# Plain f32 value products, one output bank, and side work in the gaps of an attention stage

## The chip, the cores and the metric

The kernel runs on one core of one Trainium2 chip. The metric is the time of one execution on the device in microseconds; the median of three runs is given.

## The reference, cut to what matters

```python
def _attn_ref(q, k, v):                       # q, k, v: 4 x 12 x 448 x 64, f32
    scores = scale * np.matmul(q, k.transpose(0, 1, 3, 2)) - np.log(S)
    attn = 1.0 / (1.0 + np.exp(-scores))
    return np.matmul(attn, v)
x = attn_out.transpose(0, 2, 1, 3).reshape(1792, 768)
h = x @ moe_w_in; x = elu(h) @ moe_w_out      # 768 -> 2048 -> 768
h = x @ moe2_w_in; out = (h - tanh(h)) @ moe2_w_out
```

A sigmoid takes the place of the softmax, so no row has to be normalised. The four weights arrive with 64-bit elements.

## The kernel before

**Attention.** 4 batches of 12 heads are 24 pairs of heads. For each pair `n`, TensorE transposes Q and K (`transpose`, keys `("t", n, w)`), and ScalarE and VectorE split the result into two fp32r parts whose sum is the f32 value (`head`, `rest`). Scores are then three fp32r products each. They come in four units: `u` = 0 to 2 are 128 keys of both heads at once, two 64-row halves side by side; `u` = 3 is the last 64 keys of both heads, stacked on 128 partitions. ScalarE takes the sigmoid out of PSUM (`sig`). The value products (`pv`) for `u` = 0 to 2 are plain f32, each head in 64 columns of the array. The one for `u` = 3 takes parts of sigmoid and V that were split as well (`ahead`, `arest` on VectorE, `vhead`, `vrest` on GpSimd) and is three fp32r products. VectorE copies the sum out (`xdone`). Score tiles and the transposes of the pair two turns ahead rotate through three tiles of two banks (`pss`); the value sums through two single banks (`psv`).

**The two layers.** They follow on the same tokens, in two sets (`s` = 0: 1024 tokens, `s` = 1: 768). Each layer's products go by Strassen's scheme: seven products of sums of quarters, with operands `B11, B21, T1, T2, B22, T3, T4` made from the attention output by `x_sum`, `x_head` (ScalarE) and `x_rest` (VectorE), in the places that `SLOTS` gives. Weights are narrowed from 64 bits to f32 in three steps (`narrow`, `p_narrow`: ScalarE, VectorE, VectorE). The output weights of the first layer are loaded, narrowed, summed (`p_sum`) and stored during attention (`p_load` to `p_store`, `j` = 0 to 7), four blocks of the input weights too (`load`, `narrow`, `keep`). All of this is called side work below.

**The order.** Nothing is ordered by the compiler. `Sched` holds every operation with a queue (PE, ACT, DVE, POOL, SP), a believed cost, a believed latency, what it follows and a rank. `emit` walks through time: it always takes the operation that can start first, the rank deciding between equals, and emits the program in the order of the starts so found. Each engine then runs its own operations in exactly that order, waiting on semaphores. For attention the order on each engine is fixed by `PHASES` (times within a turn of `CYCLE`) and `chain`; the products of the layers are one chain on TensorE. SyncE issues almost all DMAs, in order too.

```python
op("p_load", (j, c), "SP", 600, p_load, [("s", max(2 * j - 1, 0), 0)] + (was[c:c + 1] if wide else held), 6000)
...
raw_op(("load", n), "SP", 600, lambda: load(n, key, not live), after, 5400 if live else 3900)
```

The last number of each is the believed latency in nanoseconds.

Of the kernel before, what the change touches and what calls it, by code (L numbers as in the profile page):

```python
# [9 lines left out]
F32 = mybir.dt.float32  # L10
# [6 lines left out]
class Sched:  # L17
# [3 lines left out]
    def __init__(self):  # L21
        self.ops, self.before = {}, {}
# [8 lines left out]
    def emit(self):  # L31
        ops = self.ops
# [12 lines left out]
        while any(ready.values()):  # L45
            best = None
            for queue, keys in ready.items():
                t0 = free.get(queue, 0)
                for k, t in keys.items():
                    c = (max(t, t0), ops[k][4], str(k))  # L50
                    if best is None or c < best[0]:
                        best = c, queue, k
            (start, rank, _), queue, k = best
            del ready[queue][k]
            free[queue] = start + ops[k][1]
            done[k] = free[queue] + ops[k][5]
            order.append((start, len(order), ops[k][2]))
# [5 lines left out]
        for start, _, fn in sorted(order, key=lambda o: o[:2]):  # L63
            fn()
# [5 lines left out]
CYCLE = 6900  # L70

PHASES = {
    ("s", 0): 0, ("s", 1): 620, ("s", 2): 1240, ("s", 3): 1900, ("pv", 3): CYCLE + 2500,
    ("t", 1): 3100 - 2 * CYCLE, ("t", 0): 3500 - 2 * CYCLE, ("pv", 0): 4000, ("pv", 1): 4900, ("pv", 2): 5800,
    ("sig", 0): 700, ("sig", 1): 1700, ("sig", 2): 2700, ("sig", 3): 3700,
    ("head", 1): 4400 - 2 * CYCLE, ("head", 0): 5000 - 2 * CYCLE,
    ("ahead", 3): 4500, ("rest", 1): 5050 - 2 * CYCLE, ("arest", 3): 5100, ("rest", 0): 5700 - 2 * CYCLE,
    ("xdone",): CYCLE + 3300, ("vhead",): 1000, ("vrest",): 2000,
# [9 lines left out]
def kernel(  # L88
# [27 lines left out]
    NAN, NAH, NAF, NVL, NL = 6, 2, 2, 2, 2  # L116
# [27 lines left out]
    rooms = {tag: raw_p.tile([128, n], F32R if tag == "XA" else F32, tag=tag, name=tag) for tag, n in ROOMS.items()}  # L144
    raws = {(tag, 0): raw_p.tile([128, n], F32, tag=tag, name=tag) for tag, n in RAW.items()}
# [9 lines left out]
    with tc.manual_schedule():  # L155
# [7 lines left out]
        def attention():  # L163
# [7 lines left out]
            psv = [apool("psv0", 1, early, space=bass.MemoryType.PSUM, side="right")]  # L171
            psv += [apool("psv1", 1, space=bass.MemoryType.PSUM)]
# [4 lines left out]
            ah_p = apool("ah", NAH)  # L177
# [12 lines left out]

            vs = [vs_p.tile([128, 2, 2, D], F32R, name=f"vs{i}") for i in range(2)]
# [100 lines left out]
            def transpose(n, w):  # L292
                if ("tps", n) not in T:
                    T["tps", n] = pss[(5 * n - 6) % 3].tile([128, 2, BK], F32, tag="s", name="sps")
# [6 lines left out]
            def head(n, w):  # L301
                W, slot = ((S, 1), (512, 2))[w]
                nc.scalar.activation(out=es[n % 2][:, slot, :W], in_=T["t", n, w][:, :W], func=ACTF.Copy)  # L303
# [14 lines left out]
            def vhead(n):  # L318
# [1170 lines left out]
```

## Time and profile before

| what | value |
|---|---|
| median of three runs | 1041.16 us (1039.48 to 1042.59) |
| profiled execution | 1045.44 us, span 1043.7 us |
| TensorE matmul busy, share of the span | 998.7 us, 96% |
| VectorE busy | 779.1 us, 75% |
| ScalarE busy | 605.4 us, 58% |
| GpSimd busy | 108.8 us, 10% |
| bytes moved by DMA | 218.62 MB, mean 209 GB/s |

The span is the time from the first to the last instruction of the profiled execution. Busy shares are means over stages that differ: attention ends at about 196 us, the first layer lies up to about 625 us, the second behind it. Where TensorE is busy nearly throughout, the time of a stage is TensorE's; elsewhere one looks for what ended its idle time.

### The profile page before, as it was taken

The page shows a single profiled execution, that of the slowest core. Times are in us where ns is not written, and L with a number is a line of the kernel's source. Part 1 is how long each engine was busy: PE and PEld are TensorE (multiplying, and loading weights), DVE is VectorE, ACT ScalarE, POOL GpSimd, SP SyncE. Part 2 cuts the span into 40 slices and gives each one's busy share as a digit, 9 for nine tenths or more (in the row PEclk, how much of TensorE's full clock was granted, in tenths as well). Part 3 has the DMA queues.
Part 4 walks back from the last instruction along what each step waited for, and adds up shares of the span by engine and source line. Part 5 has one row for each costly group of instructions (what it writes and reads, how often), then busy time and mean ns, then how long its engine had stood idle before and what let it go on. Part 6 is the DMA issues. An engine that isn't in the chain of part 4 may idle for free.

```text
span 1043.7 us, 15621 instructions
## 1 busy us (share of the span) xinstructions
PE 998.7 (96%) x5276; PEld 865.4 (83%) x5276; DVE 779.1 (75%) x1135; ACT 605.4 (58%) x976; POOL 108.8 (10%) x122
## 2 busy tenths in 40 slices
PE   8887999989999999999999999899999999999998
PEld 5555666678888878888789998798898999999998
DVE  2766778797877778666878789788787788665673
ACT  4666778765556557554657655344444556445652
POOL 1001121121111110000000021132222000000000
PEclk8988999999999999999999999899999999999999
DMA  7989994044455559999995732555555895455443
GB/s 201 294 250 312 275 265 114 16 149 168 167 173 177 171 180 296 357 388 359 393 322 174 229 120 97 179 184 189 185 196 185 292 310 188 127 167 169 134 134 94
DMA packets 171264, 218.62 MB, mean 209 GB/s; under 512 B 58672, under 2 KB 129584, under 8 KB 170928
## 3 DMA queue, kind: packets, MB, share of 16 engines
q1 hardware_dynamic: 169616, 217.04, 62.9%
q8 instruction: 41, 0.67, 0.3%
q10 hardware_dynamic: 1568, 0.59, 0.2%
q14 instruction: 39, 0.32, 0.1%
HBM read 142.61 MB, written 74.97 MB: 208 GB/s over the span
## 4 chain that ended last, share of the span: by engine, by line
PE 55%; DMA 14%; DVE 12%; issue 4%; ACT 3%; SPq 1%; POOL 0%; DVEq 0%; ACTq 0%; POOLq 0%
PE psa L760 8%; PE psd L760 7%; PE psx L760 6%; DMA second<-in_moe_w_in_dram 5%; PE psu L915 4%; PE psw L915 4%; PE psv L915 4%; PE psa L915 3%; PE psb L915 3%; PE psb L760 3%; PE sps L333 3%; PE psx L915 3%; PE pvps L371 3%; DMA R1a<-in_moe_w_out_dram 2%; PE psy L915 2%
## 5 line engine op out<-in xcount | busy, mean ns | idle before, releaser
L333 PE MATMUL sps<-e 64*128 64x448 f32 (+1 forms) x504 | 74.3, 387 | 16.1 <-ACT an L347 12.8
L333 PEld LDWEIGHTS sps<-e 64*128 64x128 f32 (+1 forms) x504 | 51.7, 189 | 45.2 <-ACT an L347 20.3
L887 ACT ACTIVATE XB<-t 128x384 fp32r<-128x384 f32 (+1 forms) x111 | 61.7, 563 | 36.2 <-DMA t<-x_forms 13.5
L347 ACT ACTIVATE an<-sps,bias 128x896 f32<-128x896 f32 x72 | 67.8, 1006 | 25.4 <-PE sps L333 25.2
L891 DVE TENSOR_TENSOR XB<-t,XB 128x384 fp32r<-128x384 f32 (+1 forms) x111 | 68.0, 625 | 12.2 <-ACT XB L887 12.2
L675 POOL TENSOR_TENSOR second<-second 128x384 f32<-128x384 f32 x15 | 17.4, 1161 | 534.3 <-DVE second L562 273.7
L371 PE MATMUL pvps<-an,vl 128*64 128x448 f32 x288 | 61.7, 565 | 0.0
L760 PE MATMUL psd<-XB,R0a 128*128 128x512 f32 (+1 forms) x192 | 55.3, 369 | 4.3 <-ACT R1b L772 2.5
L760 PE MATMUL psa<-XB,W 128*128 128x512 f32 x192 | 55.2, 397 | 0.0
L887 ACT ACTIVATE XB<-spare 128x512 fp32r<-128x512 f32 (+1 forms) x72 | 40.7, 571 | 21.1 <-DMA spare<-x_forms 5.6
L891 DVE TENSOR_TENSOR XB<-spare,XB 128x512 fp32r<-128x512 f32 (+1 forms) x72 | 44.0, 621 | 6.3 <-ACT XB L887 6.3
L915 PE MATMUL psu<-XB,XB 128*128 128x384 f32 (+1 forms) x192 | 46.5, 349 | 1.4 <-DVE XB L880 1.4
L308 DVE TENSOR_TENSOR e<-sps,e 128x512 fp32r<-128x512 f32 (+1 forms) x48 | 31.2, 653 | 21.0 <-ACT e L303 19.5
L915 PE MATMUL psv<-XB,XB 128*128 128x384 f32 (+1 forms) x192 | 46.2, 348 | 0.0
L915 PE MATMUL psw<-XB,XB 128*128 128x384 f32 (+1 forms) x192 | 46.2, 348 | 0.0
L675 POOL TENSOR_TENSOR first<-first,second 128x384 f32<-128x384 f32 x30 | 43.9, 1463 | 1.2
L760 PEld LDWEIGHTS psa<-XB,W 128*128 128x128 f32 x192 | 37.0, 192 | 8.1
L760 PEld LDWEIGHTS psd<-XB,R0a 128*128 128x128 f32 x192 | 35.9, 192 | 9.0 <-ACT R1b L772 2.9
L371 PEld LDWEIGHTS pvps<-an,vl 128*64 128x64 f32 x288 | 19.2, 142 | 28.0 <-issue 23.8
L760 PE MATMUL psd<-XA,W 128*128 128x512 f32 x144 | 37.1, 403 | 3.3 <-DVE W L692 2.0
L915 PEld LDWEIGHTS psu<-XB,XB 128*128 128x128 f32 x192 | 34.6, 188 | 3.9 <-DVE XB L880 1.7
L793 ACT ACTIVATE spare<-spare 128x512 f32<-128x512 f32 (+1 forms) x64 | 36.5, 571 | 0.7
(359 smaller groups left out, 2698.8 us busy)
## 6 DMA issues: line engine op xcount, KB each, us to landing
x_forms<-R1b SPq DMA_DIRECT2D x58, 256.0 KB, 2.0
first<-p_forms SPq DMA_DIRECT2D x36, 384.0 KB, 6.5
t<-x_forms SPq DMA_DIRECT2D x64, 192.0 KB, 2.8
t<-x_forms SPq DMA_DIRECT2D x47, 256.0 KB, 4.9
x_forms<-t SPq DMA_DIRECT2D x44, 256.0 KB, 2.0
x_forms<-R1b SPq DMA_DIRECT2D x58, 192.0 KB, 5.6
first<-in_moe_w_in_dram SPq DMA_DIRECT2D x14, 768.0 KB, 5.7
second<-in_moe_w_in_dram SPq DMA_DIRECT2D x14, 768.0 KB, 7.3
```

The lines of the kernel that those rows point to most:

```text
L308: nc.vector.tensor_tensor(out=e[:, to, :W], in0=T.pop(("t", n, w))[:, :W], in1=f(e[:, slot, :W]), op=ALU.subtract)
L333: nc.tensor.matmul(out=ps[:, j, :S], lhsT=e[lanes, ks, cols], rhs=e[lanes, qs, :S], start=(x == 0), stop=(x == 2),)
L347: nc.scalar.activation(out=a[:, :m], in_=T.pop(("s", n, u))[:, :m, :S], func=ACTF.Sigmoid, bias=bias, scale=scale)
L371: nc.tensor.matmul(out=ps[D * j:D * j + D], lhsT=vl[n // NL % NVL][:, n % NL, 5 * j + u], rhs=a[:, j], start=(u == 0), stop=False,)
L675: by.tensor_tensor(out=out, in0=x, in1=y, op=op)
L760: nc.tensor.matmul(out=ps, lhsT=w[wz][:, k0:k0 + 128], rhs=xs[xz][:, kk], start=(opens and n == 0), stop=(n == 3 * KH - 1), skip_group_che ...
L793: nc.scalar.activation(out=r, in_=r, func=ACTF.Exp, scale=-1.0)
L887: nc.scalar.activation(out=at_place(og_place[i, s, p, j], 0, i)[:, :HW[s]], in_=T["graw", i, s, p, j], func=ACTF.Copy)
L891: nc.vector.tensor_tensor(out=lo, in0=T.pop(("graw", i, s, p, j)), in1=f(hi), op=ALU.subtract)
L915: nc.tensor.matmul(out=T["o2", tag], lhsT=lhsT, rhs=rhs, start=(p in OPENS and j == 0 and x == 0), stop=(j == NG - 1 and x == 2), skip_gro ...
```

## The change

- The value product of `u` = 3 becomes one plain f32 product of the sigmoid and V as loaded, in the pair's own turn. `ahead`, `arest`, `vhead`, `vrest` go, and their tiles.
- The copy `head` of Q (`w` = 0) moves from ScalarE to VectorE.
- PSUM: `u` = 3's scores get a bank of their own (`psq`); all pairs share one bank for the value sums (`psv`), so `pv` 0 of a pair follows `xdone` of the pair before. The ring `pss` has four uses a pair in place of five.
- The planner first plans attention alone (`emit(True)`). In the real planning an operation of ACT or DVE that is not in that plan is put off if it would end more than `GIVE` = 100 ns (beside the lateness that there is already) after the planned start of the next planned one.
- Believed latencies of transfers grow (`load` 8500 and 6000, `p_load` 11000, `p_store` 8000, and some loads of the layers). `p_load` no longer follows every second pair's scores, and narrowing no longer follows `head`.
- First operands of layer 1 are made in three pieces of one pair each; `XB2` is set aside from the start, and `T1`, `T2`, `B22` change places.

```diff
@@ planner
+                    if k not in plan and planned.get(queue) and c[0] + ops[k][1] > plan[planned[queue][-1]] + late + GIVE:
+                        c = (10 ** 9,) + c[1:]
...
+            start = max(ready[queue][k], free.get(queue, 0))
+            if k in plan:
+                late = start - plan[k]
...
+        if only_plan:
+            self.plan = {o[3]: o[0] for o in order}
+            return
@@ attention
-    NAN, NAH, NAF, NVL, NL = 6, 2, 2, 2, 2
+    NAN, NAF, NVL, NL = 3, 1, 2, 2
-            psv = [apool("psv0", 1, early, space=bass.MemoryType.PSUM, side="right")]
-            psv += [apool("psv1", 1, space=bass.MemoryType.PSUM)]
+            psq = apool("psq", 1, early, space=bass.MemoryType.PSUM, side="right")
+            psv = apool("psv", 1, space=bass.MemoryType.PSUM)
...
+                if w:
+                    nc.scalar.activation(out=to, in_=x, func=ACTF.Copy)
+                else:
+                    nc.vector.tensor_copy(out=to, in_=x)
...
-                    t = T.pop(("h", n, u))
-                    for vz, az in ((0, 0), (0, 1), (1, 0)):
-                        nc.tensor.matmul(
-                            out=ps, lhsT=vs[n % 2][:, vz], rhs=t[:, az], start=False, stop=(vz == 1)
-                        )
+                    nc.tensor.matmul(
+                        out=ps, lhsT=vl[n // NL % NVL][:, n % NL, 3:5], rhs=T.pop(("a", n, u))[:, 0], start=False, stop=True
+                    )
...
-                n, x = divmod(5 * n + x - 3, 5)
-                return [("sig", n, x)] if x < 4 else [("rest", n + 2, 0), ("rest", n + 2, 1)]
+                n, x = divmod(4 * n + x - 3, 4)
+                return [("sig", n, x)] if x < 3 else [("rest", n + 2, 0), ("rest", n + 2, 1)]
...
-                       + {0: loaded("v", n) + [("xdone", n - 2)], 3: [("vrest", n)]}.get(u, []))
+                    op("pv", n, (u,), "PE", 790, pv, [("sig", n, u)] + (loaded("v", n) + [("xdone", n - 1)] if u == 0 else []))
@@ layers
             def pieces(i, s):
-                return (slice(None),)
+                return (slice(None),) if i else range(KH)
...
-                raw_op(("load", n), "SP", 600, lambda: load(n, key, not live), after, 5400 if live else 3900)
+                raw_op(("load", n), "SP", 600, lambda: load(n, key, not live), after, 8500 if live else 6000)
...
-                            fixed[done] = (4 + 2 * n) * CYCLE
+                            fixed[done] = n * CYCLE
...
-                    op("p_load", (j, c), "SP", 600, p_load, [("s", max(2 * j - 1, 0), 0)] + (was[c:c + 1] if wide else held), 6000)
+                    op("p_load", (j, c), "SP", 600, p_load, [("s", 1, 0)] + (was[c:c + 1] if wide else held), 11000)
...
-                           [done] + (held + [("head", 2 * j + c + 2, 0)] if step == 0 else []), 100)
+                           [done] + (held if step == 0 else []), 100)
...
-            FIRST["XA2"] = FIRST["XB0"] = formed
+            ended = [[k for k in formed if k[1] == NG - 2 + u and (raw is None or k[0] == "p_narrow")] for u, raw in ((0, 1), (0, None), (1, 1), (1, None))]
+            FIRST["XB0"], FIRST["XA2"] = ended[0] + ended[1] + ended[3], ended[2]
...
         attention()
+        sch.emit(True)
         mlp()
         sch.emit()
```

## Rows read from the trace of the kernel before

**Rows 1.** Windows: stretch, length, busy PE, PEld, DVE, ACT, POOL, PEclk, DMA, GB/s.

```profile
10.21:189.77 179.56, 162.52 (x1004) 103.59 (x1003) 127.98 (x209) 127.44 (x177) 22.65 (x45) 0.93 0.80 240
11.30:18.20 6.90, 6.34 (x25) 3.96 (x25) 1.08 (x3) 4.83 (x7) 0.00 (x0) 0.51 0.82 184
...
51.40:56.50 5.10, 0.00 (x0) 0.00 (x0) 1.44 (x3) 2.59 (x4) 0.00 (x0) 0.92 0.78 178
56.50:62.50 6.00, 5.96 (x20) 4.27 (x22) 3.03 (x5) 3.97 (x6) 1.24 (x2) 0.50 0.75 240
...
94.46:101.16 6.70, 0.00 (x1) 0.00 (x0) 2.51 (x4) 3.66 (x6) 0.74 (x2) 0.66 0.93 301
101.16:106.90 5.74, 5.74 (x20) 4.10 (x22) 3.60 (x8) 3.70 (x6) 0.75 (x2) 0.50 1.04 343
...
196.14:225.00 28.86, 26.11 (x120) 22.70 (x119) 27.08 (x29) 21.28 (x32) 7.66 (x4) 0.94 0.19 69
217.10:223.00 5.90, 3.29 (x10) 2.74 (x9) 5.90 (x9) 4.50 (x9) 0.00 (x0) 0.71 0.49 191
...
20.00:160.00 140.00, 123.52 (x770) 79.75 (x771) 99.07 (x170) 97.17 (x134) 17.30 (x34) 0.94 0.91 281
160.00:196.00 36.00, 36.00 (x229) 22.14 (x228) 28.27 (x37) 29.73 (x43) 5.03 (x10) 1.00 0.19 52
```

**Rows 2.** The chain that ended last, one turn: start, us, what.

```profile
157.12 2.85 PE sps L333 x21
159.97 0.61 PE pvps L378 x3
160.58 0.82 PE sps L299 x8
161.40 2.41 PE pvps L371 x12
```

**Rows 3.** Timeline of ScalarE and SyncE's queue: start, us, instruction, idle before.

```profile
53.91 0.89 ACT L555 ACTIVATE R1b<-R1a 128x768 f32<-128x768 f32 x1 [5.85 <-DMA R1a<-in_moe_w_in_dram]
...
97.50 0.89 ACT L555 ACTIVATE R1b<-R1a 128x768 f32<-128x768 f32 x1 [6.33 <-DMA kept_wi<-R1b]
...
40.52 1.02 SPq L544 DMA_DIRECT2D R1a<-in_moe_w_in_dram  x1
...
94.48 0.47 SPq L574 DMA_DIRECT2D kept_wi<-R1b  x1
```

**Rows 4.** Issue to landing: input weights (L544), then output weights (L606).

```profile
DMA to landing us min/median/max: 9.4/9.7/13.3
...
DMA to landing us min/median/max: 5.0/8.2/11.4
```

**Rows 5.** VectorE groups up to 197 us: count, busy us, mean ns, idle before.

```profile
L308 DVE TENSOR_TENSOR e<-sps,e 128x512 fp32r<-128x512 f32 x24 | 16.5, 688 | 20.4 <-ACT e L303 18.9 <-PE sps L299 1.5
L308 DVE TENSOR_TENSOR e<-sps,e 128x448 fp32r<-128x448 f32 x24 | 14.8, 617 | 0.6 <-ACT e L303 0.6
L359 DVE TENSOR_TENSOR ah<-a,ah 128x448 fp32r<-128x448 f32 x24 | 14.8, 615 | 0.1
L355 DVE CAST ah<-a 128x448 fp32r<-128x448 f32 x24 | 9.7, 403 | 4.3 <-ACT a L347 3.9
...
L562 DVE SCALAR_TENSOR_TENSOR XB<-XB 128x768 int32<-128x768 int32 x8 | 7.6, 955 | 0.1
L389 DVE COPY R0a<-pvps 128x448 f32<-128x448 f32 x6 | 3.7, 623 | 6.5 <-PE pvps L378 6.5
...
L716 DVE TENSOR_TENSOR R0a<-R0a 128x1536 f32<-128x1536 f32 x2 | 3.5, 1749 | 0.0
```

**Rows 6.** Timeline of TensorE's weight loads: the fourth score product's.

```profile
159.09 0.50 PEld L333 LDWEIGHTS sps<-e 128*128 128x128 f32 x3 [0.32 <-ACT an L347]
```

**Rows 7.** VectorE groups at the seam, 196 to 222 us.

```profile
L822 DVE TENSOR_TENSOR t<-t 128x512 f32<-128x512 f32 x1 | 0.7, 678 | 0.0
```

**Rows 8.** Timeline at the seam: the weight load that waited.

```profile
219.68 0.50 PEld L760 LDWEIGHTS psd<-XB,R0a 128*128 128x128 f32 x2 [2.86 <-ACT R1b L772]
```

More of the change, by code (lines that the diff above doesn't have):

```diff
@@ L29, in chain, with emit @@
         self.before.update(zip(keys[1:], keys))
-    def emit(self):
-        ops = self.ops
+    def emit(self, only_plan=False):
+        ops, plan, late = self.ops, self.plan, 0
+        planned = {q: sorted((k for k in plan if ops[k][0] == q), key=plan.get, reverse=True) for q in ("ACT", "DVE")}
         after = {k: [a for a in o[3] if a in ops] for k, o in ops.items()}
@@ L53, in emit @@
             (start, rank, _), queue, k = best
+            start = max(ready[queue][k], free.get(queue, 0))
+            if k in plan:
+                late = start - plan[k]
+                if queue in planned:
+                    planned[queue].remove(k)
             del ready[queue][k]
@@ L56, in emit @@
             done[k] = free[queue] + ops[k][5]
-            order.append((start, len(order), ops[k][2]))
+            order.append((start, len(order), ops[k][2], k))
             for x in then[k]:
@@ L958, in mlp @@
             before_early = [(kind, last) + w for kind, w in (("rest", (0,)), ("rest", (1,)))]
[L959 to L960 removed]
+            before_early += [("s", last, u) for u in range(4)] + [("sig", last, u) for u in range(4) if u == 3 or (4 * last + u) % 3 == 0]
             before_late = [("xdone", last)]
@@ L1144, in part @@
                     r = raw[y]
-                    return r if len(ks) == 1 else [d for d in r if (d[1] % NP if i == 0 else d[3]) % KH == k]
+                    return r if len(ks) == 1 else [d for d in r if d[1] % NP % KH == k]
                 for x in ORDER:
@@ L1156, in operands @@
                             raw_op(("x_sum",) + key, by, dve(n) if by == "DVE" else int(2.6 * n) + 300,
-                                   lambda x=x, k=k: x_sum(i, s, x, k), sum((part(k, y) for y in SUMS[x]), needs[x]))
+                                   lambda x=x, k=k: x_sum(i, s, x, k), sum((part(k, y) for y in SUMS[x]), [n_ + (str(k),) for n_ in needs[x]]))
                             need = [("x_sum",) + key]
                         by = heads_on(i, s)
-                        parts_ = range(KH) if (i, s) == (0, 0) else (k,)
+                        parts_ = (k,)
                         for y in parts_:
@@ L1277, in first_out @@
                             n_r += 1
-                            op("ow_load", (0, s, p, d), "SP", 600, ow_load, raw_free[where] + [("p_store", d_, c) for d_ in (2 * d, 2 * d + 1) for c in range(2)], 4500)
+                            op("ow_load", (0, s, p, d), "SP", 600, ow_load, raw_free[where] + [("p_store", d_, c) for d_ in (2 * d, 2 * d + 1) for c in range(2)], 5000)
                             raw_free[where] = [("ow_rest", 0, s, p, d)]
```

82 lines of the change are left out of this document (31 added, 51 removed).

## The prediction

> **What bounds the kernel now.** I began with the windows view of the attention stage, because every edit that adds or removes work lies there. Between the first score product of pair 0 (10.21 us) and that of pair 23 (189.77 us) lie 23 turns in 179.56 us, 7.81 us each; TensorE is busy in 162.5 of them and VectorE in 128.0 [rows 1]. The chain of waits then shows an undisturbed turn: it is TensorE alone, scores 2.85, last value product 0.61, transposes 0.82, the other value products 2.41, together 6.69 us [rows 2]. So 179.56 - 23 x 6.69 = 25.7 us are lost to something else, and the question is what ends those waits.
>
> The reader is to see three kinds of loss. First, two standstills, 51.4 to 56.5 and 94.5 to 101.2 us, in which TensorE runs nothing (5.1 and 6.7 us); each is followed by a stretch at the lower of TensorE's two clocks, 1.2 in place of 2.4 GHz, granted 0.50 for 6.0 and 5.7 us, which gives away about 3.0 and 2.9 us more [rows 1]. Second, the cold start: 0.51 for 6.9 us, 3.4 us lost [rows 1]. Third, the other 25.7 - 17.7 - 3.4 = 4.6 us, in small waits. The timeline says what ended the standstills [rows 3]: ScalarE stood at the first step of narrowing a weight, with the sigmoids queued behind it. Once it waited 5.85 us for a weight load issued at 40.5 us, the other time 6.33 us for a store that SyncE issued only at 94.48 us. The loads of these weights take 9.4 to 13.3 us to land, where the planner believed 5.4; those of the output weights take 5.0 to 11.4, where it believed 6.0 [rows 4]. The order is written from times that the transfers do not keep.
>
> There is a second limit close behind. From 20 to 160 us the DMA engines are busy 0.91 of the time, and from 160 to 196 only 0.19 [rows 1]. Up to 160 us the kernel needs 0.91 x 140 = 127 us of their time, whatever ScalarE does. From 160 us to the seam TensorE has no gap.
>
> **Value products.** The last value product of a pair is three fp32r matmuls now, 0.61 us of TensorE [rows 2]. It becomes one plain f32 product over 128 partitions. The trace has no such form at 128 columns; the other value products are plain f32 in two 64-column halves side by side, 2.41 / 3 = 0.80 us for each block of keys [rows 2]. Bounds: 0.61 (no dearer than before) and 1.61 (as dear as two blocks); I take 0.80, the nearest row, since one full-width product streams the same 448 columns as a pair of halves does. That is +0.19 us a pair.
>
> VectorE loses the cast, 0.40, and the subtraction, 0.62, a pair [rows 5], 24 x 1.02 = 24.5 us; GpSimd loses its two casts of V, which nobody on the path waited for. One copy of Q's transpose goes from ScalarE to VectorE, which already copies 448 f32 columns out of PSUM in 0.62 [rows 5]: VectorE +14.9 us over 24 pairs. All this lies beside TensorE's 6.69 and counts nothing by itself.
>
> **Banks.** The fourth score product gets a bank of its own. Before, it shared a ring with the first, and its weight load stood 0.32 us until that sigmoid had read its bank [rows 6]. I take 0.32 off a turn (bounds 0 and 0.32). The turn becomes 6.69 + 0.19 - 0.32 = 6.56 us; over 24 pairs -3.1 us (bounds: +24 x 1.0 if the product costs 1.6 and the wait stays, -7.7 if it costs nothing more).
>
> The value products share one output bank, so the first of the next pair waits for the copy-out. Between the last product of a pair and that first one stand four scores and the transposes, 2.53 + 0.82 = 3.35 us; the copy takes 0.62 [rows 5]. Even with a 0.96 us narrowing step ahead of it on VectorE, 1.6 us fit. Cost nothing; without the cover it would be 0.62 a pair, 15 us.
>
> **Planner.** Loads are now believed to take 8.5 and 11 us, and work beside attention goes only where it delays a planned instruction by at most 0.1 us. For the output weights 11 covers nearly all landings of up to 11.4 [rows 4]; I halve the small waits, -2.3. For the first weights 8.5 covers neither the median 9.7 nor the longest 13.3: the 5.85 us wait loses 8.5 - 5.4 = 3.1 and becomes 2.75, as long as the 2.5 us wait at the seam that did cost some clock [rows 1, 8], so I keep half of the clock loss: -3.1 - 1.5. The wait for the store has no edit of its own; it only moves, because narrowing is ranked earlier. I take half, -3.3 - 1.4 (bounds 0 and -9.6). Sum of the waits: 2.3 + 4.6 + 4.7 = 11.6, with the turn 14.7 us.
>
> **The DMA cap.** That sum assumes that the transfers keep up. No DMA is removed. The side work must still run from 20 us on, and 127 us of DMA time in the stretch that took 140 lets it shrink by 12.6 at a share of 1.0, which the trace reaches over 5.7 us (1.04 at 101 us) [rows 1], and by 8.7 at 0.97, half way between the two. I take 12.6, and 5.4 turns of the cheaper kind behind it, 0.7: attention ends 13.3 us sooner, not 14.7.
>
> **First operands.** They go to pieces of 512 or 384 columns, so that a block begins when the first of its three pairs is out. A whole subtraction of 1536 takes 1.75 us [rows 5], one of 512 takes 0.68 [rows 7], three of them 2.04: each split costs 0.29 of VectorE, 22 of them at most 6.4, hidden in VectorE's idle time as long as that lasts. At the seam VectorE is full, 27.1 of 28.9 us, and TensorE stands 2.5 us at 217 because ScalarE could not yet write a temporary [rows 1, 8], with a granted clock of 0.71 over the 5.9 us there [rows 1], 1.7 lost. Pieces, and a buffer that no longer waits for the end of attention, move part of these subtractions ahead of the seam. Worth 0 to 4.2; I take 2.0.
>
> **Sum.** -13.3 - 2.0 = -15.3 us. The profiled execution took 1045.44 us, with 1.7 outside its span of 1043.7; it would take 1030.1. The median of the runs shown is 1041.16, 4.3 lower, so the forecast for the median is 1025.9, 1026.
>
> **Rivals.** *The waits go altogether (0.15).* If packets stretch each other while they queue, 127 us overstates the need and the cap is soft. Then all of 25.7 but the cold 3.4 goes, with 3.1 from the turn and 4.2 at the seam: -29.6, 1012. For it: the share is 0.91 on average, not 1. Against it: the landings that are already late.
>
> *The waits come back elsewhere (0.18).* A landing of 13.3 against a belief of 8.5 is 4.8 us late; with the store's 6.7 and the clock behind both (5.9) that is 17.4 of the 17.7 again. Only the turn's 3.1 and some small waits are won, 1033 to 1040. For it: output weights are no longer paced by every second pair, so the planner may ask for them sooner than the DMA engines can deliver.
>
> *Side work starves the seam (0.13).* This is the slower one. A turn leaves VectorE 6.56 - (0.62 + 0.62 + 0.69 + 0.62) = 4.0 us, 96 us over 24 pairs. The side work before the seam is 128.0 - 23 x (1.02 + 0.69 + 0.62 + 0.62), some 60 us, so 0.62 of those gaps must be filled, with steps of up to 0.96 us and little leave to overrun. What is not filled comes after the seam, where VectorE has 1.8 us free in 28.9, and there a microsecond late is a microsecond of TensorE. With 15.3 us unfilled (gaps filled to 0.47) nothing is won; filled to 0.40, 22 us late, the time is 1041 + 7 = 1048.
>
> *One bank binds (0.04).* If the copy-out stood on the path, 0.62 a pair, 15 us, would eat the 15.3 won: 1041, no change. The 3.35 us in between speak against it. The Trainium skill, "TensorEngine Tiling (Array Packing)", PSUM Bottleneck, warns that packing speeds up TensorE but not the evacuation of PSUM, whose copy may become the bottleneck. By that rule the time would be this rival's; the trace so far shows VectorE idle before these copies, waiting for the last value product [rows 5].
>
> **How the numbers follow.** The forecast has 0.50; its own range is 1022 (14.7 and 4.2 won) to 1032 (a DMA share of 0.97 and nothing at the seam). The range 1011 to 1041 takes in the two faster-side cases to their ends and leaves out the starved seam. A measurement of this kernel tells about 0.3%, 3.1 us, from no change. Faster: 0.50 + 0.15 + 0.15 of the returning waits = 0.80. Same: 0.03 of these and 0.03 of the bank, 0.06. Slower: 0.13 and 0.01 of the bank, 0.14.
>
> **What would show it.** Right: turns of about 6.56 us without disturbance, the wait before the fourth score gone, no stretch of half clock after the cold start or one short one, the seam at about 183 us of the span, a DMA share near 1 up to 147 us. Wrong: the last value product above 1 us (then the turn is slower), ScalarE still standing 5 us at a narrowing step, the first value product of a pair waiting for VectorE, or TensorE idle for 10 us at the seam. Behind attention I expect the same time; a difference there of more than 3 us, from the later beliefs about the loads of the two layers, would break the sum too.

## The result and the profile after

The changed kernel takes 1023.88 us in the median (1022.43 to 1025.52, four runs), the kernel before beside it 1040.32 us (1036.18 to 1042.59, four runs): a ratio of 0.9847, 95% interval 0.9811 to 0.9883, or 16.4 us less. The forecast was 1026. Its parts did not come out that way, and the rest of this document is about that.

The stages, from the first product of each to that of the next, in the two profiled executions (before's was 5.1 us above its median, after's 0.7 below):

| stage | before, us | after, us | difference | forecast |
|---|---|---|---|---|
| start to the first product of layer 1 (attention) | 196.3 | 187.7 | -8.6 | -13.3 |
| layer 1, input weights | 217.9 | 210.9 | -7.0 | -2.0 (the seam) |
| layer 1, output weights | 208.2 | 203.5 | -4.7 | 0 |
| layer 2, input weights | 211.7 | 209.8 | -1.9 | 0 |
| layer 2, output weights | 205.6 | 205.6 | 0 | 0 |
| span | 1043.7 | 1021.5 | -22.2 | -15.3 |

More than half of what was won in these two executions lies behind attention, where only the seam's 2.0 us were forecast. Line numbers moved: L544, L555, L574, L760 of before are L536, L547, L566, L752 of after.

Windows of after, the columns as in [rows 1]: attention from the first score product of pair 0 to that of pair 23; the stretch in which before had its first standstill; the one standstill that is left and the half clock around its end; the 37 us from the seam on, and the stop and the half clock in them; 20 to 160 us.

```profile
10.04:181.95 171.91, 163.70 (x982) 94.42 (x982) 114.76 (x198) 114.76 (x150) 0.00 (x0) 0.98 0.84 250
51.40:62.50 11.10, 11.10 (x70) 6.43 (x66) 7.71 (x14) 4.98 (x7) 0.00 (x0) 1.00 0.99 327
88.55:95.30 6.75, 0.00 (x1) 0.00 (x0) 0.54 (x1) 1.47 (x3) 0.00 (x0) 0.86 1.06 322
93.43:100.26 6.83, 4.96 (x20) 3.29 (x20) 3.74 (x6) 3.88 (x6) 0.00 (x0) 0.50 1.06 317
187.70:225.00 37.30, 30.59 (x140) 26.76 (x139) 35.38 (x61) 27.52 (x54) 4.72 (x4) 0.91 0.20 69
209.41:215.85 6.44, 0.00 (x0) 0.00 (x0) 6.44 (x13) 3.71 (x7) 0.00 (x0) 0.77 0.21 81
212.90:219.72 6.82, 3.87 (x12) 3.87 (x13) 6.82 (x14) 2.30 (x5) 0.00 (x0) 0.50 0.47 181
20.00:160.00 140.00, 132.38 (x797) 76.97 (x797) 94.26 (x164) 94.58 (x123) 0.00 (x0) 0.98 0.92 278
```

Against [rows 1]: the first standstill and the cold stretch of half clock are gone, the second standstill is as long as it was (6.75 for 6.70 us), and at the seam TensorE stands 6.44 us in place of 2.54. The half clock there lasts 6.8 us, from 212.9 to 219.7; it begins inside the stop, and TensorE works in 3.87 us of it. In before it lay behind the stop, from 219.5 to 223.0 us, with TensorE at work in 3.25 us of it. The DMA share from 20 to 160 us is 0.92; it was 0.91.

One undisturbed turn in the chain of after, beside [rows 2], and from the timeline the weight loads of the fourth score product and of the last value product:

```profile
154.77 2.03 PE sps L344 x18
156.79 0.81 PE spq L344 x3
157.61 0.82 PE sps L309 x8
158.43 2.41 PE pvps L370 x12
160.84 0.95 PE pvps L376 x2
```
```profile
156.72 0.51 PEld L344 LDWEIGHTS spq<-e 128*128 128x128 f32 x3 [0.31 <-issue]
160.77 0.30 PEld L376 LDWEIGHTS pvps<-a,vl 128*128 128x128 f32 x2 [0.70 <-issue]
```

The turn is 7.02 us, slower than before's 6.69; 6.56 was forecast. The fourth score product has its own bank and its weight load still stands 0.31 us, as [rows 6] showed with a shared one; only the releaser's name is gone. The last value product takes 0.95 us.

What ended the standstill that is left: ScalarE and SyncE's queue in after, beside [rows 3].

```profile
61.45 0.89 ACT L547 ACTIVATE R1b<-R1a 128x768 f32<-128x768 f32 x1 [3.38 <-DMA R1a<-in_moe_w_in_dram]
...
93.83 0.89 ACT L547 ACTIVATE R1b<-R1a 128x768 f32<-128x768 f32 x1 [6.99 <-DMA kept_wi<-R1b]
...
69.92 5.62 SPq L234 DMA_DIRECT2D first<-in_q_dram  x4
...
86.19 0.42 SPq L566 DMA_DIRECT2D kept_wi<-R1b  x1
```

The wait for the weight load is down from 5.85 to 3.38 us, and TensorE runs through it. The wait for the store is longer than the 6.33 us of before: SyncE issues it at 86.19 us, in the middle of loads of Q, K and V.

The seam in after, in the order VectorE, GpSimd, ScalarE, TensorE (timeline):

```profile
192.68 1.49 DVE L724 TENSOR_TENSOR R0a<-R1a,R0a 128x384 fp32r<-128x384 f32 x3
197.97 3.13 DVE L724 TENSOR_TENSOR R0b<-R1a,R0b 128x384 fp32r<-128x384 f32 x3
213.78 1.49 DVE L724 TENSOR_TENSOR R1a<-R1b,R1a 128x384 fp32r<-128x384 f32 x3
...
198.27 1.14 POOL L667 TENSOR_TENSOR second<-second 128x384 f32<-128x384 f32 x1 [194.92 <-DMA second<-kept_wi]
...
215.31 0.49 ACT L764 ACTIVATE R1b<-psd 128x384 f32<-128x384 f32 x1 [2.06 <-DVE R1a L724]
...
215.85 1.01 PE L752 MATMUL psd<-XB,R0a 128*128 128x384 f32 x2 [6.44 <-ACT R1b L764]
```

TensorE's stop ends with ScalarE's copy into R1b, which waited for VectorE to finish the last operand of the second token set, at 215.3 us. VectorE is busy throughout the stop. Three subtractions of 384 columns took 3.13 us while GpSimd added weights, 1.49 otherwise.

Now the layers. Lines L544 (before) and L536 (after) are the weight loads; this is who waited for them in layer 1 (us in total, times) and how long they took to land, before and then after. The loads into `first` belong to the stage of the input weights; those into `R1a` and `R1b` are issued in the stage of the output weights, for layer 2:

```profile
who waited for it (us, times):
  ACT R1b L555: 26.4, 8
  ACT R1a L555: 18.6, 7
  ACT first L555: 14.9, 5
...
DMA to landing us min/median/max: 4.7/7.2/10.0
```
```profile
who waited for it (us, times):
...
DMA to landing us min/median/max: 4.6/6.9/8.4
```

No engine waits for them any more, though they land about as late. Before, the planner believed 5.4 us for loads that are narrowed, now 8.5. What such a wait did to TensorE is seen in one place of before's timeline:

```profile
375.08 0.91 ACT L555 ACTIVATE first<-second 128x768 f32<-128x768 f32 x1 [3.88 <-DMA second<-in_moe_w_in_dram]
...
376.03 0.56 DVE L558 TENSOR_SCALAR first<-first 128x768 int32<-128x768 int32 x1 [2.63 <-ACT first L555]
376.62 0.96 DVE L562 SCALAR_TENSOR_TENSOR second<-second,first 128x768 int32<-128x768 int32 x1
377.50 0.68 DVE L777 TENSOR_TENSOR t<-t,psa 128x512 f32<-128x512 f32 x1
...
378.23 0.73 PE L760 MATMUL psa<-XB,e 128*128 128x512 f32 x2 [1.99 <-DVE t L777]
```

ScalarE stands 3.88 us for a load, VectorE behind it, VectorE's addition out of bank `psa` stands behind the narrowing, and TensorE waits 1.99 us for that bank. Windows of layer 1 behind the seam, before and then after:

```profile
225.00:414.20 189.20, 180.78 (x882) 158.87 (x881) 148.74 (x213) 114.26 (x203) 31.21 (x24) 1.00 0.57 191
```
```profile
225.00:398.60 173.60, 173.60 (x863) 156.02 (x862) 139.92 (x208) 112.34 (x199) 34.86 (x24) 1.00 0.61 205
```

8.4 us of idle TensorE before, none after.

### The profile page after: what moved, and what is told of

Its sections match the earlier page's. It is cut to its first block, busy times and chain, and to the rows that moved or that the text cites. A ratio compares the mean times of both kernels' runs of the same rounds, so it can differ in the third digit from the quotient of the medians.

```text
span 1021.5 us, 15446 instructions
## 1 busy us (share of the span) xinstructions
PE 994.0 (97%) x5252; PEld 857.2 (84%) x5252; DVE 766.8 (75%) x1155; ACT 601.9 (59%) x966; POOL 79.9 (8%) x74
## 4 chain that ended last, share of the span: by engine, by line
PE 93%; DVE 4%; DMA 1%; issue 1%; ACT 1%; SPq 0%; DVEq 0%; ACTq 0%
PE psa L752 12%; PE psd L752 11%; PE psx L752 9%; PE psu L907 7%; PE psw L907 7%; PE psv L907 7%; PE psa L907 6%; PE psb L907 6%; PE pvps L370 5%; PE psb L752 5%; PE sps L344 5%; PE psy L907 4%; PE psx L907 3%; PE pvps L376 2%; PE sps L309 2%; PE spq L344 2%
## 5 line engine op out<-in xcount | busy, mean ns | idle before, releaser
L370 PE MATMUL pvps<-an,vl 128*64 128x448 f32 x288 | 59.4, 548 | 0.0
L344 PEld LDWEIGHTS sps<-e 64*128 64x128 f32 x432 | 40.2, 190 | 19.2 <-issue 15.6
L752 PE MATMUL psa<-XB,W 128*128 128x512 f32 x192 | 55.3, 398 | 0.0
L344 PE MATMUL sps<-e 64*128 64x448 f32 x432 | 52.1, 382 | 0.6 <-DVE e L322 0.6
L752 PEld LDWEIGHTS psa<-XB,W 128*128 128x128 f32 x192 | 37.0, 193 | 7.9
L781 ACT ACTIVATE spare<-t 128x512 f32<-128x512 f32 (+1 forms) x33 | 19.0, 578 | 39.2 <-DVE t L769 38.3
L317 DVE CAST e<-sps 128x448 fp32r<-128x448 f32 x24 | 15.0, 625 | 35.4 <-PE sps L309 25.7
L370 PEld LDWEIGHTS pvps<-an,vl 128*64 128x64 f32 x288 | 18.6, 136 | 26.0 <-issue 22.2
L752 PE MATMUL psd<-XB,W 128*128 128x512 f32 x144 | 37.1, 403 | 3.3 <-DVE W L684 2.0
L667 POOL TENSOR_TENSOR first<-first,second 128x384 f32<-128x384 f32 x30 | 40.0, 1334 | 1.2
L907 PE MATMUL psa<-XB,XB 128*128 128x384 f32 (+1 forms) x156 | 36.9, 347 | 0.0
L907 PE MATMUL psb<-XB,XB 128*128 128x384 f32 (+1 forms) x156 | 36.9, 347 | 0.0
```

The source lines that it names most:

```text
L344: nc.tensor.matmul(out=ps[:, j, :S], lhsT=e[lanes, ks, cols], rhs=e[lanes, qs, :S], start=(x == 0), stop=(x == 2),)
L370: nc.tensor.matmul(out=ps[D * j:D * j + D], lhsT=vl[n // NL % NVL][:, n % NL, 5 * j + u], rhs=a[:, j], start=(u == 0), stop=False,)
L667: by.tensor_tensor(out=out, in0=x, in1=y, op=op)
L752: nc.tensor.matmul(out=ps, lhsT=w[wz][:, k0:k0 + 128], rhs=xs[xz][:, kk], start=(opens and n == 0), stop=(n == 3 * KH - 1), skip_group_che ...
L781: nc.scalar.activation(out=r, in_=h, func=ACTF.Tanh)
L907: nc.tensor.matmul(out=T["o2", tag], lhsT=lhsT, rhs=rhs, start=(p in OPENS and j == 0 and x == 0), stop=(j == NG - 1 and x == 2), skip_gro ...
```

## The experiments

Each was timed against the kernel before on the same chip; ratios are to that. "Attention" is the time of layer 1's first product.

**The product alone.** Before, with the one plain f32 product in the old place and two output banks.

```diff
-                    for vz, az in ((0, 0), (0, 1), (1, 0)):
-                        nc.tensor.matmul(out=ps, lhsT=vs[n % 2][:, vz], rhs=t[:, az], ...)
+                    nc.tensor.matmul(out=ps, lhsT=vl[...][:, n % NL, 3:5], rhs=T.pop(("a", n, u))[:, 0], ...)
```

> The kernel before with the value product alone changed: one plain f32 product in its old place, right behind the fourth scores, in the old two banks. Theory: the product costs 0.95 us in the changed kernel because its 128-column weights cannot be loaded while the 64-column halves still run; behind the full-width scores it costs 0.75 to 0.80, so the undisturbed turn goes from 6.69 to about 6.85 us and the time rises by about 4 us if the standstills stay (1044). Rival: the form costs 0.95 wherever it stands, turn 7.03, about 8 us more (1048). A second rival: without the VectorE steps the standstills shrink, and the time falls below 1036.

1038.22 us, ratio 0.9983 (0.9958 to 1.0007): no difference that can be told. Its chain:

```profile
165.71 2.83 PE sps L333 x21
168.54 0.75 PE pvps L376 x2
169.30 0.82 PE sps L299 x8
170.12 2.41 PE pvps L371 x12
```

Here the product takes 0.75 us, against 0.95 in after: it follows full-width scores, and its weight load ran beside them. In after it follows blocks in 64 columns, and the load stands 0.70 us ([0.70 <-issue] above) and runs in front of it. The turn is 6.81 us, and attention still ends at 198.6: less work on VectorE did nothing for the standstills. The three stages behind it took 214.3 + 205.2 + 209.4 us, 8.9 less than in before's profile, with no belief changed; before's profiled execution is a slow one, and differences against it can come out too large.

**The belief about weight loads alone.** Before, with one line changed.

```diff
-                raw_op(("load", n), "SP", 600, lambda: load(n, key, not live), after, 5400 if live else 3900)
+                raw_op(("load", n), "SP", 600, lambda: load(n, key, not live), after, 8500 if live else 6000)
```

> The kernel before with one number pair changed: the believed latency of the weight loads, 8500 and 6000 in place of 5400 and 3900. Theory: most of the 13.6 us that the two layers won comes from this alone (ScalarE no longer stands at narrowing steps for late loads); from the first product of layer 1 to the last product 843 us become 831 or less, and the first standstill of attention shrinks too, total 1022 to 1030. Rival: the places, pieces or the other beliefs did it; the layers stay within 3 us of 843.

1026.94 us, ratio 0.9874 (0.9843 to 0.9905). Attention ends at 198.3, 2.0 later than before; the gain is in the layers, 206.3 + 204.2 + 208.7 for 217.9 + 208.2 + 211.7 us. Put in alone, one line gives 13.7 us (1040.59 for the kernel before beside it), where the whole change gave 16.4, and none of it where I looked. Taken out of the changed kernel, in the next experiment, it costs half of that.

**The changed kernel without that belief.** The same line back at 5400 and 3900.

> The changed kernel with the believed latency of the weight loads back at 5400 and 3900. Theory: the layers lose what they won, from 830 us to about 840, and a standstill of 4 to 6 us at a narrowing step in attention comes back; total 1035 to 1042. Rival: the layers stay at 830 and the total within 4 us of 1024.

1030.63 us, ratio 0.9907 (0.9876 to 0.9937), 6.75 us above after and below the 1035 to 1042 expected. Attention is as in after (187.6), without the expected new standstill; layer 1's input weights take 218.5 for 210.9 us. ScalarE again waits for the loads; its waits in the stages of the input and of the output weights (us in total, times, longest), and the window of the latter:

```profile
ACT first L547 <- DMA second<-in_moe_w_in_dram: 11.1, 5, 2.9
...
ACT R1a L547 <- DMA R1a<-in_moe_w_out_dram: 23.7, 7, 4.4
ACT R1b L547 <- DMA R1b<-in_moe_w_out_dram: 16.5, 8, 4.0
```
```profile
406.20:609.60 203.40, 203.40 (x1018) 183.53 (x1018) 157.23 (x226) 123.25 (x201) 6.11 (x4) 1.00 0.84 305
```

Put in and taken out, the belief moves layer 1's input weights by 11.6 and 7.6 us: it is a cause of the gain there. In the output weights' stage ScalarE waits 40.2 us again, and the stage takes 203.5 us as in after, with TensorE busy throughout: these waits cost nothing there. What shortened that stage from 208.2 us is open.

**A later belief about the stores of narrowed input weights.** After, with 12.0 us in place of 5.6, so that the planner expects the store that ends the standstill later.

```diff
-                    raw_op(("keep", n, key), "SP", 600, lambda: keep(n, key), [done], 5600)
+                    raw_op(("keep", n, key), "SP", 600, lambda: keep(n, key), [done], 12000)
```

> The changed kernel with the believed latency of the store of kept weights at 12000 in place of 5600. Theory: the one standstill left in attention (6.75 us at 88.6 us, ScalarE at a narrowing step behind that store) goes, and the half clock behind it, 3.4 us: the first product of layer 1 at 178 us in place of 187.7, total about 1014. Rival, the cap of the prediction: the DMA engines are full up to 150 us, so the wait comes back at another narrowing step, and the first product of layer 1 comes no sooner than 184 us.

1033.12 us, ratio 0.9930 (0.9911 to 0.9949), slower than after. That wait went and another came, 50 us later, for a store of output weights, which SyncE issued at 131.75 us. From 118.9 us on its queue had held almost nothing but loads of Q, K and V; since when the store's data were ready is not shown:

```profile
121.36 4.56 SPq L217 DMA_DIRECT2D kq<-in_k_dram  x3
...
131.75 0.43 SPq L612 DMA_DIRECT2D p_forms<-XB  x1
...
140.95 0.89 ACT L547 ACTIVATE XB<-XB 128x768 f32<-128x768 f32 x1 [7.36 <-DMA p_forms<-XB]
...
142.79 1.86 PE L309 MATMUL sps<-ident,kq 128*128 128x128 f32 x8 [5.12 <-ACT an L358]
```

Side work ended later (the last of these stores was issued at 171.2 us, in after at 159.4), and layer 1's input weights took 217.8 us. A belief later than the transfer (7.6 us to land in after) was no cure here; the order changed elsewhere too.

**Whole operands for the second token set.** After, where only the first set's operands come in pieces.

```diff
             def pieces(i, s):
-                return (slice(None),) if i else range(KH)
+                return (slice(None),) if i or s else range(KH)
```

> The changed kernel with the operands of the second token set made whole again (the first set still in pieces). At the seam of the changed kernel TensorE stands 6.4 us because VectorE has 27 us of work behind the end of attention in place of 22.5. Theory: it is the side work that moved there, and pieces only add fixed costs of 0.14 us each; whole operands end VectorE's queue about 1.5 us sooner, the wait falls to about 5 us, the total by 1 to 2 us. Rival: pieces start the operands sooner and are worth more than they cost; whole, the wait grows to 8 us or more and the total rises by 2 us or more.

1020.75 us, ratio 0.9826 (0.9793 to 0.9858). At the seam TensorE waits 1.94, 1.50 and 2.61 us in place of 6.44 at once, nothing is granted at half clock, attention ends at 186.1 and the stage behind takes 209.4. The intervals of this kernel and of after overlap; by the spans (1018.1 for 1021.5) the second set's pieces cost some 3 us, 1.5 of them in the stage behind the seam.

**No rule about gaps.** After, with `GIVE` so large that the rule never applies.

```diff
-GIVE = 100
+GIVE = 10 ** 9
```

> The changed kernel without the rule on gaps (the leave to overrun is without limit). Theory: side work is placed as soon as it is ready, planned attention instructions are pushed, and attention's turns grow irregular, 7.1 to 8 us; the first product of layer 1 comes 3 to 8 us later than 187.7, but less work is left behind the seam, so the wait there falls from 6.4 to under 4; total within 5 us of 1024. Rival: the rule is what made the turns regular and the standstills rare; without it two or more standstills of over 4 us return and the total is above 1032.

1028.44 us, ratio 0.9899 (0.9867 to 0.9931). Attention ends at 198.9, 11.2 later than in after, with one long standstill, behind two of ScalarE's waits for loads, 4.10 and 7.53 us:

```profile
66.04 0.89 ACT L547 ACTIVATE R1b<-R1a 128x768 f32<-128x768 f32 x1 [7.53 <-DMA R1a<-in_moe_w_in_dram]
...
68.67 1.86 PE L309 MATMUL sps<-ident,first 128*128 128x128 f32 x8 [10.24 <-ACT an L358]
```

The seam, in turn, is nearly clean: waits of 1.18 and 0.92 us, and 204.6 for 210.9 us in the stage behind it. So the rule wins 11.2 us in attention and hands 6.3 to the seam. The theory was the nearer of the two: the total is within 5 us of after, though attention lost more than the 3 to 8 us expected.

**The last value product behind the next pair's scores.** After, with one bank, but the product and the copy-out in the old place.

```diff
-    ..., ("pv", 2): 5800, ("pv", 3): 6500,
+    ..., ("pv", 2): 5800, ("pv", 3): CYCLE + 2500,
-    ..., ("xdone",): CYCLE + 500,
+    ..., ("xdone",): CYCLE + 3300,
```

> The changed kernel with the last value product of a pair moved behind the fourth scores of the next pair, where it stood before; still one f32 product and one output bank. The run of the product alone showed a turn of 6.81 us there, so the product costs about 0.74 us behind full-width scores and 0.95 behind the 64-column halves. Theory: the turn falls from 7.02 to 6.82 to 6.88, about 4 us less over the stage, if the copy-out of 0.62 us fits behind the transposes of 0.82. Rival: with one output bank the copy-out no longer fits, the first value product waits for it, and the turn stays at 7.0 or more.

1029.45 us, ratio 0.9902 (0.9869 to 0.9936). The turn is 6.82 us, 0.20 less than in after, and the first value product waits for the copy-out in two turns only, 0.19 and 0.18 us, with 0.82 us of transposes between them. But three standstills of 5.6, 4.8 and 3.3 us came back, behind ScalarE's waits for stores of 8.57, 5.88 and 5.39 us. The dearer place wins all the same, by 5.6 us in medians and by what the order around it becomes; which of the shifted steps does that I did not isolate.

**All side-work stores on GpSimd's queue.** After, with the stores of narrowed input weights and of output weights issued by GpSimd.

```diff
-                nc.sync.dma_start(out=kept[key], in_=result(job))
+                nc.gpsimd.dma_start(out=kept[key], in_=result(job))
...
-                nc.sync.dma_start(out=p_forms()[:, a0:a1, j], ...)
+                nc.gpsimd.dma_start(out=p_forms()[:, a0:a1, j], ...)
```

> The changed kernel with the stores of attention's side work (kept weights and summed output weights) issued by GpSimd in place of SyncE. Theory: both standstills seen so far (6.75 us in the changed kernel, 5.1 us with the longer belief) were ended by stores that stood in SyncE's queue behind loads of Q and K, which wait for their buffers; on a queue of their own they leave when their data are ready, no standstill above 2 us is left, and the first product of layer 1 comes at 177 to 181 us in place of 187.7; total 1013 to 1018. Rival: the stores are late because the DMA engines are full; the standstill stays and the total is within 3 us of 1024.

1026.53 us, ratio 0.9870 (0.9824 to 0.9915): no better than after. Attention ends at 182.1, 5.6 sooner, with one standstill of 3.21 us left, behind ScalarE's wait of 5.75 for a weight load; the seam stands 3.79 us at 191 and 6.60 at 210 us, and the stage there takes 216.9 for 210.9. What attention won was given back there. The profiled execution was the fastest of four (1020.94 us); what the others lost beyond that is not shown.

**The product and the belief together.** The edits of the first two experiments, in before.

> The kernel before with two edits alone: the full-width f32 value product, in its old place behind the next pair's scores and with two output banks, and the believed latency of 8.5 and 6.0 us for the weight loads. Theory: most of the gain is the belief's, in the layers, and the product's in the first of them; the two add, 2.1 and 13.4 us: some 1025 (1022 to 1029), attention ending at about 198, no better and no worse than the whole change. Rival: the gaps, the one bank and the pieces pay as well, and the sum of two edits stays over 1029. Second rival: beliefs shift the whole order, so sums of single edits tell nothing; then 1035 or 1015 is as likely.

1029.71 us, ratio 0.9887 (0.9842 to 0.9933): the median lies just above 1029, as the first rival had it, and no better than the belief alone. The two single ratios together, 0.9857, still lie in the interval, so that they do not add is not shown. Attention ends at 196.8 with stops of 7.57, 3.68 and 2.82 us. The miss is 5 us; the sum of single edits was no better than that here, as the second rival warned.

With this run there are three pairs that differ in the believed latency of the loads alone (us; the last column is how long ScalarE waits for weight loads in each of the three stages):

| kernel | belief | layer 1, input | layer 1, output | layer 2, input | waits |
|---|---|---|---|---|---|
| before | 5.4 | 217.9 | 208.2 | 211.7 | 14.9, 45.0, 11.2 |
| before, belief | 8.5 | 206.3 | 204.2 | 208.7 | none |
| before, product | 5.4 | 214.3 | 205.2 | 209.4 | 10.7, 35.5, 7.4 |
| before, product and belief | 8.5 | 208.4 | 204.8 | 209.8 | none |
| after without the belief | 5.4 | 218.5 | 203.5 | 210.9 | 11.1, 40.2, 7.6 |
| after | 8.5 | 210.9 | 203.5 | 209.8 | none |

In layer 1's input weights the belief is worth 11.6, 5.9 and 7.6 us; in the output weights 4.0, 0.4 and 0, although ScalarE's waits are longest there.

**Fewer bytes.** After, with two of seven forms of the output weights stored, the order unchanged.

```diff
-                nc.sync.dma_start(out=p_forms()[:, a0:a1, j], in_=t[:, :(a1 - a0) * DH]...)
+                a1 = a0 + 1
+                nc.sync.dma_start(out=p_forms()[:, a0:a1, j], in_=t[:, :DH]...)
...
-                ..., in_=p_forms()[:, FORMS.index(W_OF[p]), 2 * d:2 * d + 2])
+                ..., in_=p_forms()[:, min(FORMS.index(W_OF[p]), 1), 2 * d:2 * d + 2])
```

> The changed kernel, with two of the seven forms of the first layer's output weights stored (their loads later read these two), so the summed forms never leave the core and the output is not the reference's: 7.9 MB of about 39 MB that move between 20 and 160 us are left out, the order of every queue stays. Theory: the standstill of 6.75 us at 88.6 us comes from SyncE's order (a store behind loads that wait for buffers) and stays within 2 us; attention ends at 186 to 188. Rival: it comes from the DMA engines' capacity; with the share falling from 0.92 to about 0.75 the loads land in 6 to 7 us, buffers come free sooner, and the standstill goes, with the half clock behind it: attention ends at 178 to 180, total 8 to 10 us less, 1014 to 1016.

1018.72 us, ratio 0.9784 (0.9739 to 0.9828). Attention ends at 184.1. The window of 20 to 160 us, and ScalarE's wait in the timeline:

```profile
20.00:160.00 140.00, 135.76 (x819) 79.29 (x817) 96.78 (x169) 95.62 (x124) 0.00 (x0) 0.98 0.80 233
```
```profile
90.07 0.89 ACT L547 ACTIVATE R1b<-R1a 128x768 f32<-128x768 f32 x1 [5.13 <-DMA kept_wi<-R1b]
```

Between the two expectations, nearer to the order: with the share down from 0.92 to 0.80 TensorE's standstill is still 4.24 us (6.75), so bytes explain some 2.5 us of it, more than the 2 us that the theory allowed.

**More leave for side work.** Whole operands for the second set, and `GIVE = 600`.

> The changed kernel with the second token set's operands whole and a leave of 0.6 in place of 0.1 us for work beside attention. Theory: side steps last 0.6 to 1.0 us and gaps on VectorE are shorter, so the rule with 0.1 us leaves work for the seam; with 0.6 the seam's waits fall from 6.1 to about 3 us and attention ends less than 3 us later than 186.1: 1018 to 1020, by some 2 us better than with 0.1. Rival: what counts is ScalarE's order; with more leave the narrowing steps stand before sigmoids again whenever a transfer is late, standstills of 5 to 10 us come back as without the rule, attention ends at 190 to 199, total 1024 to 1028.

1026.59 us, ratio 0.9853 (0.9813 to 0.9893). The rival was right: attention ends at 194.3 with waits of 5.33 and 9.82 us on ScalarE, and the seam won 1 us for it.

**Only the two stores of input weights on GpSimd's queue.** Whole operands for the second set, and the first half of the queue edit above.

> The changed kernel, with the second token set's operands whole, and the two stores of narrowed input weights issued by GpSimd, so that they don't stand in SyncE's queue; all else as with whole operands alone. Theory: the standstill of 5.70 us at 87.8 us is the store's place in SyncE's order (issued at 84.56 us, 7.3 us to land, ScalarE behind it 6.59 us); issued as soon as the weight is narrowed, it has landed when ScalarE comes; the standstill falls under 2 us and the half clock behind it goes, attention ends at 178 to 181 and the rest stays: 1011 to 1015. Rival: what attention wins is given back, as it was with all stores on GpSimd: another transfer is late in its place, or the seam waits 5 us longer; 1018 to 1022.

1014.88 us (1014.27 to 1017.64), ratio 0.9767 (0.9744 to 0.9790). It beats both kernels, and its interval lies clear of after's and, by a hair, of that with whole operands alone (0.9793 to 0.9858). GpSimd's first issue, ScalarE's wait, the longest of TensorE's standstills that is left in attention (the next is 1.25 us), and the window, in this order:

```profile
63.72 0.71 POOL L566 DMA_DIRECT2D kept_wi<-R1b  x1 [60.35 <-DVE R1b L554]
...
77.67 0.89 ACT L547 ACTIVATE R1b<-R1a 128x768 f32<-128x768 f32 x1 [4.68 <-DMA R1a<-in_moe_w_in_dram]
...
79.50 1.04 PE L309 MATMUL sps<-ident,kq 128*128 128x128 f32 x8 [2.15 <-ACT an L358]
```
```profile
20.00:160.00 140.00, 136.59 (x838) 79.33 (x836) 98.41 (x171) 98.32 (x129) 1.26 (x2) 1.00 0.94 289
```

The store goes out at 63.72 us, as soon as VectorE has written its data; with whole operands alone SyncE issued it at 84.56 (86.19 in after). The standstill falls from 5.70 to 2.15 us, the half clock behind it is gone, attention ends at 181.5 in place of 186.1. The theory held, each figure at or just past its edge. The rest stayed within 1.3 us a stage of whole operands alone, though the profiled execution was the slowest of five (1017.64 us).

## Why the prediction came out as it did

The time was right, 1026 for 1023.88, and the sum behind it was not. The turn and the seam came out with the wrong sign, 10.7 and 6.2 us worse than their terms, and a term that was set to nothing made up for them. That the total fits is luck; in the two profiled executions, from which the sum was built, 22.2 us went and not 15.3.

**The step that failed: nothing behind attention.** The prediction said that the layers keep their time and that a difference of more than 3 us would break the sum. It was 17.8 us in the profiled executions: -7.0 - 4.7 - 1.9, and 4.2 more because the seam, which is counted in the first of these, got worse. I had read the landings of weight loads in attention alone [rows 4], and costed their belief there. The same line orders the loads of layer 1, where they took 4.7 to 10.0 us, 7.2 in the median, against a belief of 5.4, and ScalarE stood 59.9 us for them (26.4 + 18.6 + 14.9). The trace of before showed that; I did not ask it.

Those 59.9 us are not what the waits cost. 45.0 of them lie in the output weights' stage, and after without the belief has 40.2 us of them there with TensorE never idle. In the input weights' stage the waits reach TensorE, and three pairs of runs settle the belief as a cause, worth 5.9 to 11.6 us. The 4.7 us of the output weights and the 1.9 of layer 2 are not traced to it. Part of the 17.8 is likely before's profiled execution itself, 5.1 us above its median; the product alone, with no belief changed, had 8.9 us less in these stages. 8.4 are idle time in layer 1's input weights, 2.8 in its output weights; part of the rest lies in time that the trace counts as busy. In medians the belief was worth 13.7 us put in alone and 6.75 taken out.

**Value products: mis-sized.** 0.80 us was taken, from bounds of 0.61 and 1.61; it is 0.95 in its new place and 0.75 in the old. The term's row had its weight loads hidden; in the new place the load stands in front of the product. The old place gave 0.75 in the changed kernel too (the turn of 6.82 us), so the place is what costs 0.20.

**The fourth score's bank: no gain.** The 0.32 us were put down to a bank that another score shared, by the releaser that [rows 6] names. With a bank of its own the stop stays, 0.31 us. The load is the first over 128 rows behind products in 64-row halves. The Trainium skill, "TensorEngine Tiling (Array Packing)", Key Properties, says that a change of the tiling mode drains TensorE. The trace agrees in that the stop of 0.31 us here and that of 0.70 in front of the last value product both stand at such a change; the change from the transposes to the 64-column products, in the same turn, shows 0.14 us at most. In the old place the last value product has full-width neighbours, and its load does not stand. For the stop of 0.31 us no run took the change of mode away, so that cause is only argued. With both terms the turn is 7.02 and not 6.56 us: +7.6 over 23 turns for a forecast of -3.1 over 24.

**Waits in attention: better than forecast.** What the turns do not explain fell from 25.7 to 171.91 - 23 x 7.02 = 10.5 us, by 15.2, where 11.6 was forecast; 3.4 of it is the cold half clock, which the forecast left in. The wait for the load went further than forecast (no stop of TensorE, where half a clock loss was left: 8.1 us for 4.6), and the small waits went from 4.6 to about 1.2. But the belief, to which the sum put the load's term, did not do it: put in alone it left a standstill of 5.59 us at 50.6 us, and without it the changed kernel has no stop there either and attention ends at the same time (187.6 for 187.7). Without the gap rule a standstill of 10.24 us stands there and attention ends 11.2 us later, so the rule carries most of what was won; of the other edits in attention none was tried by itself. The wait for the store was to halve, and its standstill and half clock still cost 9.2 us of 9.6. Why the cold half clock went I did not test.

**The DMA cap: not the limit.** It was to hold the attention stage 1.4 us above what the waits gave. The fastest version moved 289 GB/s at a share of 0.94 with no stop over 2.2 us, and a sixth fewer bytes (233 for 278 GB/s) left 4.24 of 6.75 us of the standstill. What held the store was in the main its place in SyncE's order; moved out of it, the store was on time.

**One bank: right.** No first value product waits for the copy-out in after; in the version that copies later two do, 0.2 us each. The rival with the rule from the Trainium skill, "TensorEngine Tiling (Array Packing)", PSUM Bottleneck, is not what happened: evacuation did not become the bound.

**The seam: the slower rival in part.** -2.0 was forecast; it is 3.9 us more standing (6.44 for 2.54) and 0.3 more lost to the clock (half of the 3.87 us in which TensorE worked at half clock, for half of 3.25), +4.2. The place and the mechanism are those of the starved seam: VectorE is full and side work that the gaps refused lies behind attention (the stage is 6.3 us shorter without the rule). The price was 4.2 and not 22. Part of it is the pieces of the second set: whole, the stage is 1.5 us shorter and has no half clock.

**Waits that come back elsewhere** was the rival to take more seriously. It did not decide this change, yet four experiments ended so (the later belief about stores, the product in its old place, the two edits together, and more leave).

## What to carry to other kernels

A belief in a planner's table is used in every stage that shares its line: before costing an edit of it, ask the trace who waits for those transfers in each stage, and then whether the engine that sets the time waits for that: 40 us of ScalarE's waits cost nothing in one stage here, 11 us cost 7.6 in another. In an order written ahead, a store that frees a buffer must not stand in a queue behind loads that wait for buffers; two stores on another queue were worth 5.3 to 5.9 us here in medians (against the kernel before beside each run, or directly). The two changes of a belief that were tried alone brought that stage nothing: attention ended 2.0 and 1.2 us later. And a forecast that hits the total should still be taken apart by stage, since here three wrong terms made a right sum.

## What the runs showed of the hardware

- The same full-width f32 product of 448 columns took 0.75 us behind full-width products and 0.95 behind products in 64 columns of the array; its weight load is hidden in the one case, and in the other it stands 0.70 us and then takes 0.30.
- The first weight load over the full array behind products in 64-row halves stood 0.31 us with a bank of its own and 0.32 with a shared one. The load for 64-row halves behind 64-column products stood 0.70 us in 20 turns of before.
- While GpSimd added blocks of 384 columns (1.14 us and more each), three VectorE subtractions of 384 took 3.13 in place of 1.49 us (two of them 1.36 and 1.38 in place of 0.55). The Trainium skill, "GPSIMD Engine Reference", Specifications, names contention with VectorE instructions that have two SBUF inputs. These have two, and the trace agrees.
- The clock was granted at half for 6.8 us around the end of a single stop of 6.44 us, from 3.5 us into it. With whole operands the same stage stood 1.94, 1.50 and 2.61 us with work between, and the clock was granted at 1.00 from 200 to 220 us. With two stores on GpSimd's queue it stood nearly the same, 1.94, 1.51 and 2.64 us, and half the clock was granted for 3.4 us. No run shows what tells these two apart.
